# Seven quarter products for eight in the fp32 projection of a fused attention and SwiGLU kernel

## Chip, cores, metric

One NeuronCore of one Trainium2 chip. The metric is the device time of one execution in microseconds (us). Before the change it is 719.2 us (719.14 to 719.45). Each run of a changed kernel was made on the same chip as runs of the kernel before; the kernel before has medians of 718.9 to 719.2 us on these chips.

## The reference

```python
# attention: B=4, H=8, S=768, D=48; per head a state that decays by w
for t in range(S):
    cur = einsum('bhd,bhe->bhde', u * k[t], v[t])
    y[t] = einsum('bhd,bhde->bhe', r[t], state + cur)
    state = w[:, :, None] * state + einsum('bhd,bhe->bhde', k[t], v[t])
x = y.transpose(0, 2, 1, 3).reshape(3072, 384)
# feed-forward: d_model 384, d_ff 1536
g = x @ w_gate
h = (g * sigmoid(g)) * (x @ w_val)
return (h @ w_out).astype(float32)
```

The last product, `h @ w_out`, is what the change touches.

## The kernel before

The sequence is cut into 24 units of 128 tokens. The attention of unit s runs in step s. Two units make a group of 256 tokens, and the feed-forward of a group is cut into items that fill PE's gaps between the parts of the attention: twelve gate-and-value items and six projection items per group.

```python
def gate_value(g, f):                       # one item: 128 of the 1536 hidden columns
    gv = ps_f.tile([P, 2, 2 * P], FP32, name="gv", tag="gv")        # two PSUM buffers
    ...                                     # 3 + 3 matmuls of 256 columns
    act.activation(sg[:], gv[:, 0, :], AF.Sigmoid)
    dve.tensor_mul(sg[:], sg[:], gv[:, 0, :])
    dve.tensor_mul(hT[g][:, f, :], sg[:], gv[:, 1, :])              # frees gv

def project(g, j, part):                    # unit j of the group, a third of it
    ...
    for f in range(4 * part, 4 * part + 4):
        pe.matmul(ps[:], hT[g][:, f, P * j : P * (j + 1)], wo[:, f, :],   # 384 columns
                  start=(f == 0), stop=(f == FC - 1))
    if part == 2:
        act.copy(o_sb[:], ps[:])
        act.dma_start(out=out[n0 : n0 + P, :], in_=o_sb[:])
```

A step begins with work on POOL whose result DVE reduces. DVE takes its instructions in program order, so whatever follows `du` in the program waits with it:

```python
def own_product(i):
    pool.tensor_mul(rk[:], rl[:], kl[:])
    pool.tensor_mul(rk[:], rk[:], ub[:])
    dve.tensor_reduce(du[:], rk[:], axis=AX.X, op=ALU.add)

for s in range(3, N + 2):                   # conditions and queue() left out
    diagonal(s - 1)
    own_product(s + 1); scale(s + 1)        # POOL: rk, rk, khat, rhat
    turn(s); gaps(s, 0)                     # PE: two transposes tp; then fill items
    scores(s - 1, 0); gaps(s, 1)            # PE: s_ps; DVE: copy_predicated into At
    scores(s - 1, 1); gaps(s, 2)
    outputs(s - 2); gaps(s, 3)              # PE: y_ps
    update(s - 2); gaps(s, 4)               # PE: u_ps; DVE and POOL: Z
```

The tiles tp, s_ps, y_ps and u_ps share four PSUM banks. Steps 3 to 11 have few fill items (a step takes 13 us); later steps have twelve.

## Time and profile before

| | before |
|---|---|
| median time | 719.2 us |
| PE busy, share of the span | 97% |
| POOL busy, share | 21% |
| projection instructions on PE | 576, one per 322.5 ns |
| PE waits after 142 us | 0.6 us in all |

The lines behind this table stand in the prediction below. The page's first part gives each engine's busy time. Its second part cuts the span into 40 slices, with the busy share in tenths; `PEclk` is the clock granted to PE. A line of the timeline is start, length, engine, source line, operation, tiles, count. In brackets stands the idle time ahead of it with what ended it.

### The profile page before, as it was taken

To read this page: it belongs to the slowest core of one execution; us is meant where nothing else is said; L and a number is where in the kernel's file an instruction comes from. 1 tells how busy PE (TensorE), PEld (TensorE's weight loads), DVE (VectorE), ACT (ScalarE), POOL (GpSimd) and SP (SyncE) were. 2 spreads that over 40 slices of the span, in tenths; PEclk is the share of its full clock that TensorE was granted. 3 is DMA by queue.
4 is the path that set the end of the run, shared out by engine and by line. 5 is a ranking of instruction groups with operands and counts; after the bars stand their busy time and mean duration, and the time that the engine had idled before them with its cause. 6 is when DMAs were issued, how large, how long until landed. Compare 5 with 4: busy or idle time off the path is not lost.

```text
span 717.4 us, 10610 instructions
## 1 busy us (share of the span) xinstructions
PE 697.7 (97%) x4390; PEld 561.6 (78%) x4390; DVE 224.3 (31%) x479; ACT 202.2 (28%) x498; POOL 148.7 (21%) x143
## 2 busy tenths in 40 slices
PE   8878999999999999999999999999999999999996
PEld 8767888878778778788778788778778778778773
DVE  5777773312222223122213123213122213112120
ACT  3577764441213022313112212113122212111010
POOL 6877673250202020202020202020100000000000
PEclk9999999999999999999999999999999999999999
DMA  8798822121201010100111010110100000000000
GB/s 235 196 233 230 214 50 56 37 60 26 45 12 25 21 36 10 34 22 13 33 24 22 23 33 12 34 23 1 24 12 2 11 12 1 12 12 0 12 13 26
DMA packets 85770, 34.02 MB, mean 47 GB/s; under 512 B 76368, under 2 KB 79568, under 8 KB 85712
## 3 DMA queue, kind: packets, MB, share of 16 engines
q1 hardware_dynamic: 82256, 28.52, 17.2%
q10 hardware_dynamic: 3456, 4.72, 1.9%
q8 instruction: 37, 0.61, 0.4%
q14 instruction: 21, 0.17, 0.1%
HBM read 28.51 MB, written 4.72 MB: 46 GB/s over the span
## 4 chain that ended last, share of the span: by engine, by line
PE 86%; DVE 5%; ACT 5%; POOL 2%; issue 1%; DMA 1%; SPq 0%; DVEq 0%; POOLq 0%
PE gv L390 47%; PE o_ps L408 26%; PE y_ps L344 5%; PE s_ps L314 4%; PE tp L300 2%; ACT At L291 2%; PE u_ps L357 1%; ACT w_mag L162 1%; ACT kT L303 1%; DVE At L318 1%; DMA r_ld<-in_r_dram 1%; DVE wg L180 1%; DVE hT L398 1%; POOL At L285 1%; DVE wg L179 0%
## 5 line engine op out<-in xcount | busy, mean ns | idle before, releaser
L390 PE MATMUL gv<-xT,wg 128*128 128x256 f32 x864 | 212.3, 382 | 0.0
L390 PE MATMUL gv<-xT,wv 128*128 128x256 f32 x864 | 210.0, 379 | 0.0
L408 PE MATMUL o_ps<-wo,hT 128*128 128x384 f32 x576 | 198.0, 488 | 0.6 <-ACT o_sb L414 0.6
L397 DVE TENSOR_TENSOR sg<-sg,gv 128x256 f32<-128x256 f32 x144 | 60.5, 420 | 414.4 <-ACT sg L396 414.0
L390 PEld LDWEIGHTS gv<-xT,wg 128*128 128x128 f32 x864 | 160.0, 190 | 31.9 <-issue 1.8
L390 PEld LDWEIGHTS gv<-xT,wv 128*128 128x128 f32 x864 | 164.2, 190 | 22.3
L396 ACT ACTIVATE sg<-gv 128x256 f32<-128x256 f32 x144 | 55.1, 383 | 366.9 <-PE gv L390 366.8
L408 PEld LDWEIGHTS o_ps<-wo,hT 128*128 128x128 f32 x576 | 106.9, 190 | 63.7 <-issue 2.0
L370 POOL TENSOR_TENSOR Z<-Z,wL 96x384 f32<-96x384 f32 x16 | 15.9, 996 | 347.9 <-DVE Z L369 347.9
L398 DVE TENSOR_TENSOR hT<-sg,gv 128x256 f32<-128x256 f32 x144 | 60.5, 420 | 4.9
L291 ACT ACTIVATE At<-ident,du 128x128 f32<-128x128 f32 x176 | 53.6, 390 | 0.5 <-ACT o_sb L414 0.5
L314 PEld LDWEIGHTS s_ps<-rT,kT 96*128 96x128 f32 x384 | 49.2, 192 | 4.3 <-DVE At L318 1.6
L314 PE MATMUL s_ps<-rT,kT 96*128 96x128 f32 x384 | 50.5, 275 | 1.7 <-DVE At L318 1.3
L344 PE MATMUL y_ps<-At,v_ld 128*32 128x128 f32 x768 | 36.1, 279 | 6.5 <-ACT kT L303 5.2
L318 DVE COPY_PREDICATED At<-mask,s_ps 128x512 f32<-128x512 int32 x48 | 35.0, 731 | 5.0 <-PE s_ps L314 4.9
L344 PEld LDWEIGHTS y_ps<-At,v_ld 128*32 128x32 f32 x768 | 29.9, 111 | 7.5 <-ACT kT L303 5.6
L344 PE MATMUL y_ps<-rT,Z 96*32 96x128 f32 x480 | 30.2, 278 | 2.1 <-ACT kT L303 2.1
L414 ACT COPY o_sb<-o_ps 128x384 f32<-128x384 f32 x24 | 11.5, 479 | 72.7 <-PE o_ps L408 72.7
L303 ACT ACTIVATE kT<-tp,own 96x512 f32<-96x512 f32 x48 | 30.0, 675 | 3.6 <-PE tp L300 3.6
L162 ACT ACTIVATE w_mag<-w_bits 128x384 f32<-128x384 f32 x36 | 19.0, 528 | 24.9 <-DVE wg L180 10.8
L202 POOL TENSOR_TENSOR rk<-r_ld,k_ld 128x384 f32<-128x384 f32 x24 | 24.4, 1019 | 4.4 <-DMA r_ld<-in_r_dram 4.4
L344 PEld LDWEIGHTS y_ps<-rT,Z 96*32 96x32 f32 x480 | 19.3, 109 | 7.6 <-issue 4.6
(57 smaller groups left out, 347.4 us busy)
## 6 DMA issues: line engine op xcount, KB each, us to landing
k_ld<-in_k_dram SPq DMA_DIRECT2D x24, 192.0 KB, 2.8
r_ld<-in_r_dram SPq DMA_DIRECT2D x24, 192.0 KB, 3.5
w_bits<-in_moe_w_gate_dram SPq DMA_DIRECT2D x6, 768.0 KB, 5.1
v_ld<-in_v_dram SPq DMA_DIRECT2D x48, 96.0 KB, 2.8
w_bits<-in_moe_w_val_dram SPq DMA_DIRECT2D x6, 768.0 KB, 5.0
w_bits<-in_moe_w_out_dram SPq DMA_DIRECT2D x6, 768.0 KB, 4.5
out_dram<-o_sb ACTq DMA_DIRECT2D x24, 192.0 KB, 1.9
ub<-in_u_dram SPq DMA_DIRECT2D x1, 192.0 KB, 4.2
```

The source lines that it names most:

```text
L162: act.activation(mags[n][-1].bitcast(FP32), hi.bitcast(FP32), AF.Abs, scale=float(2.0**-112))
L202: pool.tensor_mul(rk[:], rl[:], kl[:])
L291: act.activation(At[i % 2][:, h, :], ident[:], AF.Identity, scale=du[:, h : h + 1])
L303: act.activation(kT[i % 2][:, :, e, :], tp[0:D2], AF.Identity, scale=own[:, e : e + 1])
L314: pe.matmul(ps[:, n, :], kT[i % 2][:, a, e, :], turned[i][:, a, :], start=True, stop=True, skip_group_check=True,)
L318: dve.copy_predicated(At[i % 2][:, 4 * half : 4 * half + 4], mask[:].bitcast(INT32).unsqueeze(1).to_broadcast([P, HP, P]), ps[:],)
L344: pe.matmul(ps[32 * q : 32 * q + 32, cc, :], *rows[q][n], start=(n == 0), stop=(n == len(rows[q]) - 1), skip_group_check=True,)
L390: pe.matmul(gv[:, o, :].rearrange("p (i t) -> p i t", i=2), wt[:, c, P * f : P * (f + 1)], xT[:, 2 * g % NX : 2 * g % NX + 2, c, :], start ...
L396: act.activation(sg[:], gv[:, 0, :], AF.Sigmoid)
L397: dve.tensor_mul(sg[:], sg[:], gv[:, 0, :])
L398: dve.tensor_mul(hT[g][:, f, :], sg[:], gv[:, 1, :])
L408: pe.matmul(ps[:], hT[g][:, f, P * j : P * (j + 1)], wo[:, f, :], start=(f == 0), stop=(f == FC - 1),)
```

## The change

The projection of a group is a product of a 256 x 1536 matrix by a 1536 x 384 one. Cut in quarters it takes eight products of 128 x 768 by 768 x 192. A form of Strassen's algorithm needs seven, with sums of quarters on both sides: four weight sums (once; one of them overwrites its quarter, `w12`) and four hidden sums per group. Everything stays fp32. The sums go to POOL, those of the last group to DVE.

```diff
+    def weight_sums():
+        pool.tensor_sub(wt[1][:], w22, w12)
+        pool.tensor_sub(w12, w12, w11)
+        pool.tensor_sub(wt[0][:], w22, w12)
+        pool.tensor_sub(wt[2][:], w21, wt[0][:])
+    def h_sums(g, by):
+        ...
+        by.tensor_add(s1, h22, h21)
+        by.tensor_sub(s2, s1, h11)
+        by.tensor_sub(s3, h11, h21)
+        by.tensor_sub(s4, h12, s2)
...
-    def project(g, j, part):
-        for f in range(4 * part, 4 * part + 4):
-            pe.matmul(ps[:], hT[g][:, f, P * j : P * (j + 1)], wo[:, f, :], ...)
+    def project(g, n):                     # product n of seven, accumulators a and b
+        ...
+        lhs, rhs, acc = ((h11, w11, "a"), (h12, w21, "b"), (s2, wt[0], "a"), (s3, wt[1], "a"),
+                         (s1, w12, "b"), (h22, wt[2], "a"), (s4, w22, "b"))[n]
+        for f in range(FH):
+            pe.matmul(ps[:], lhs[:, f, :], rhs[:, f, :], ...)      # 192 columns
+        ...                                # 4 ACT copies and 3 DVE adds per group
...
+            todo.append((NW + 1, lambda: h_sums(0, pool)))         # a fill item; so for each group
...
         gaps(s, 4)
         if s == 12:
             count_outside()
+        if done["pool"] == NW and not summed:
+            summed.append(True)
+            weight_sums()                  # at the end of step 7, ahead of the next rk
```

More of the change, by code (lines that the diff above doesn't have):

```diff
@@ L398, in gate_value @@
         dve.tensor_mul(hT[g][:, f, :], sg[:], gv[:, 1, :])
-    o_ps = {}
-    def project(g, j, part):
-        c, b = divmod(2 * g + j, B)
-        if part == 0:
-            o_ps[g, j] = ps_o.tile([P, DM], FP32, name="o_ps", tag="o")
-        ps = o_ps[g, j]
-        for f in range(4 * part, 4 * part + 4):
+    FH, NH = FC // 2, DM // 2
+    w11, w12, w21, w22 = (
+        wo[:, FH * k : FH * (k + 1), NH * n : NH * (n + 1)] for k in range(2) for n in range(2)
+    )
+    wt = [cst.tile([P, FH, NH], FP32, name=f"wt{n}") for n in (2, 3, 4)]
@@ new lines, in weight_sums, with h_quarters @@
+    def weight_sums():
[3 more added lines that the diff above has]
+        pool.tensor_sub(wt[2][:], w21, wt[0][:])
+    part_of = {}
+    def h_quarters(g):
+        return [
+            hT[g][:, FH * k : FH * (k + 1), P * j : P * (j + 1)] for j in range(2) for k in range(2)
+        ]
+    def h_sums(g, by):
+        a, b = (
+            three.tile([P, 2, FH, P], FP32, name=n, tag="w_bits") for n in ("hs12", "hs34")
+        )
+        h11, h12, h21, h22 = h_quarters(g)
+        s1, s2, s3, s4 = a[:, 0], a[:, 1], b[:, 0], b[:, 1]
+        by.tensor_add(s1, h22, h21)
+        by.tensor_sub(s2, s1, h11)
+        by.tensor_sub(s3, h11, h21)
+        by.tensor_sub(s4, h12, s2)
+        part_of[g] = {"s": (s1, s2, s3, s4)}
@@ new lines, in project @@
+    def project(g, n):
+        h11, h12, h21, h22 = h_quarters(g)
+        x = part_of[g]
+        if n == 0:
+            x["a"] = ps_o.tile([P, NH], FP32, name="o_a", tag="o")
+            x["b"] = ps_w.tile([P, NH], FP32, name="o_b", tag="w_mag")
+            x["out"] = [two.tile([P, DM], FP32, name="o_sb", tag="o_sb") for _ in range(2)]
+        s1, s2, s3, s4 = x["s"]
+        lhs, rhs, acc = (
+            (h11, w11, "a"), (h12, w21, "b"), (s2, wt[0], "a"), (s3, wt[1], "a"),
+            (s1, w12, "b"), (h22, wt[2], "a"), (s4, w22, "b"),
+        )[n]
+        ps = x[acc]
+        for f in range(FH):
@@ L408, in project @@
             pe.matmul(
-                ps[:], hT[g][:, f, P * j : P * (j + 1)], wo[:, f, :],
-                start=(f == 0), stop=(f == FC - 1),
-            )
-        if part == 2:
-            o_sb = two.tile([P, DM], FP32, name="o_sb", tag="o_sb")
-            act.copy(o_sb[:], ps[:])
+                ps[:], lhs[:, f, :], rhs[:, f, :],
+                start=(f == 0 and n in (0, 1, 4)), stop=(f == FH - 1), skip_group_check=True,
+            )
+        o1, o2 = x["out"]
+        if n in (0, 2, 3):
+            nm = {0: "p1", 2: "u2", 3: "u3"}[n]
+            x[nm] = two.tile([P, NH], FP32, name=nm, tag=nm)
+            act.copy(x[nm][:], ps[:])
+        elif n == 1:
+            dve.tensor_add(o1[:, 0:NH], x["p1"][:], ps[:])
+        elif n == 4:
+            dve.tensor_add(o2[:, NH:DM], x["u3"][:], ps[:])
+        elif n == 5:
+            act.copy(o2[:, 0:NH], ps[:])
+        else:
+            dve.tensor_add(o1[:, NH:DM], x["u2"][:], ps[:])
@@ L415, in project @@
+        if n >= 5:
+            j = 6 - n
+            c, b = divmod(2 * g + j, B)
             n0 = S * b + P * c
-            act.dma_start(out=out[n0 : n0 + P, :], in_=o_sb[:])
+            act.dma_start(out=out[n0 : n0 + P, :], in_=x["out"][j][:])
+    summed = []
     todo = []
@@ L422, in feed @@
         for _ in range(n):
-            ready = [k for k, (need, _) in enumerate(todo) if need <= done["pool"]]
+            ready = [k for k, (need, _) in enumerate(todo) if need <= done["pool"] + len(summed)]
             if ready:
@@ L427, in queue @@
     def queue(g):
-        parts = [(NW, lambda p=p: project(g - 1, p // 3, p % 3)) for p in range(6)] if g > 1 else []
+        parts = [(NW + 1, lambda p=p: project(g - 1, p)) for p in range(7)] if g > 1 else []
         if g == 2:
-            todo.extend((NW, lambda p=p: project(0, p // 3, p % 3)) for p in range(6))
+            todo.append((NW + 1, lambda: h_sums(0, pool)))
+            todo.extend((NW + 1, lambda p=p: project(0, p)) for p in range(7))
         for f in range(FC):
-            need = 2 * (f // 2) + 2 if g < 2 else NW
+            need = 2 * (f // 2) + 2 if g < 2 else NW + 1
             todo.append((need, lambda f=f: gate_value(g, f)))
-            if parts and 2 <= f < 8:
+            if parts and f == 0:
+                todo.append((NW + 1, lambda: h_sums(g - 1, pool)))
+            if parts and 2 <= f < 9:
                 todo.append(parts.pop(0))
@@ L509, in fast @@
             count_outside()
+        if done["pool"] == NW and not summed:
+            summed.append(True)
+            weight_sums()
     assert done["pool"] == NW
     feed(len(todo))
-    for p in range(6):
-        project(N // 2 - 1, p // 3, p % 3)
+    h_sums(N // 2 - 1, dve)
+    for p in range(7):
+        project(N // 2 - 1, p)
 @with_exitstack
```

## The prediction

> **What bounds the kernel now.** I read the page's busy shares first, then the slices and the chain of waits, to see whether one engine sets the end throughout.
>
> ```profile
> PE 697.7 (97%) x4390; PEld 561.6 (78%) x4390; DVE 224.3 (31%) x479; ACT 202.2 (28%) x498; POOL 148.7 (21%) x143
> PE   8878999999999999999999999999999999999996
> POOL 6877673250202020202020202020100000000000
> PEclk9999999999999999999999999999999999999999
> PE 86%; DVE 5%; ACT 5%; POOL 2%; issue 1%; DMA 1%; SPq 0%; DVEq 0%; POOLq 0%
> L408 PE MATMUL o_ps<-wo,hT 128*128 128x384 f32 x576 | 198.0, 488 | 0.6 <-ACT o_sb L414 0.6
> ```
>
> PE is full in every slice after the sixth. The list of waits from 142 us to the end holds only one wait of PE, 0.6 us, between the last two units. So after 142 us a microsecond of PE work taken out is a microsecond of the end, unless it returns as a wait. The projection is 576 instructions. POOL, which gets the new work, is idle most of the time, but it is in order, and so is DVE behind it.
>
> The 488 ns of the row is latency; what counts is the spacing of starts. I took it from PE's timeline in a full stretch:
>
> ```profile
> 403.51 2.74 PE L408 MATMUL o_ps<-wo,hT 128*128 128x384 f32 x8
> 406.09 0.84 PE L357 MATMUL u_ps<-v_ld,khat 128*96 128x96 f32 x8
> 406.76 1.49 PE L390 MATMUL gv<-xT,wg 128*128 128x256 f32 x6
> ...
> 420.60 1.06 PE L314 MATMUL s_ps<-rT,kT 96*128 96x128 f32 x8
> 421.49 2.75 PE L408 MATMUL o_ps<-wo,hT 128*128 128x384 f32 x8
> ```
>
> (406.09-403.51)/8 = 322.5 ns for 384 columns; 0.67/8 = 84 ns for 96; 0.89/8 = 111 ns for 128; L390 (six in 1.29 to 1.30 us, next rows) 215.8 ns for 256. The line through 256 and 384 is 0.833 ns per column plus 2.5 ns, and 96 and 128 lie within 2 ns of it.
>
> **What the Trainium skill says.** (1) "TensorE: Matmul & The Clock Gate", section "Back-to-back issue gap": an isolated warm matmul takes N/2.4 + 2.5 ns. Here the slope is twice that (322.5 ns = 2 x 384/2.4 + 2.5), and each matmul of the program stands as two instructions in the trace (576 for 288). That fits (2) "FP8 and Floating Point Precision", section "TensorE Precision Notes": true FP32 is four passes. So fp32 is stream bound, with almost no fixed part, and halving the columns halves the time. The weight load is a separate 190 ns record, but s_ps starts every 111 ns with a new 128-column stationary each time, so at 162 ns it stays hidden. (3) "GPSIMD Engine Reference", section "Elementwise — side-by-side cycle accounting": a two-input fp32 operation of 2048 elements took 4497 ns. The trace agrees in rate: 384 elements take 1.01 us (L202 to L275), 768 int32 ones 1.87 us (L190). (4) the first page, section "What's actually happening": an idle window of about 3.4 us halves PE's clock. The trace shows it: PE is idle from 51.0 to some 55.6 us, and the stretch 56 to 58 us has a granted clock of 0.50.
>
> **The change, part by part.**
>
> *Removed and added on PE.* Before, a group is 2 units x 12 blocks x 2 instructions = 48 at 322.5 ns = 15.48 us. After, 7 products x 6 blocks x 2 = 84 at 192 columns, 0.833 x 192 + 2.5 = 162.5 ns, = 13.65 us. That is 1.83 us a group, 12 groups: **-22.0 us**.
>
> *Evacuation.* One ACT copy of 384 columns per unit (0.479 us) becomes four ACT copies and three DVE adds of 192 per group, about 0.32 and 0.35 us each (my scaling of 256 in 0.383 and 0.420). Both engines are under a third busy. There is one buffer per accumulator, so product 3 must wait for the copy after product 2 on the same one. In the built order there is in nearly all groups a gate-and-value item (2.59 us of PE) or attention work between them. The tightest are three groups where eight diagonal activations and three copies stand before that ACT copy: it ends some 5.0 us into the step and is needed at 5.4. The last group has the products adjacent and pays about 0.55 us, as the old one did between its units. I allow **+0.7 us** for all of it.
>
> *Sums of hidden tiles on POOL.* Four operations of 768 elements, some 1.8 us each with 0.1 us after a dependent one: 7.4 us a group. From group 1 on I placed them by the built order: they stand after that step's scaling work, or at the end of a step in which khat and rhat for the next are already made, and product 2 comes over 10 us later. Nothing waits. The last group's run on DVE (about 0.9 us each): sums 1 and 2 end 3.4 us after PE's last gate-and-value matmul, and products 0 and 1 cover 3.9 us.
>
> *Weight sums, once.* Four operations of 1152 elements, about 2.6 us each (estimate from the 384 and 768 rows), with dependences 10.7 us. They stand on POOL between Z and the next rk, when the last chunk of wo is rounded. This is where I looked at POOL and DVE together:
>
> ```profile
> 104.09 0.99 POOL L370 TENSOR_TENSOR Z<-Z,wL 96x384 f32<-96x384 f32 x1 [0.92 <-DVE Z L369]
> 105.04 0.99 POOL L202 TENSOR_TENSOR rk<-r_ld,k_ld 128x384 f32<-128x384 f32 x1
> 106.11 1.00 POOL L203 TENSOR_TENSOR rk<-rk,ub 128x384 f32<-128x384 f32 x1
> ```
>
> ```profile
> 107.15 0.55 DVE L205 TENSOR_REDUCE du<-rk 128x8 f32<-128x384 f32 x1 [0.31 <-POOL rk L203]
> 107.62 0.73 DVE L318 COPY_PREDICATED At<-mask,s_ps 128x512 f32<-128x512 int32 x1
> 110.33 0.42 DVE L397 TENSOR_TENSOR sg<-sg,gv 128x256 f32<-128x256 f32 x1 [1.97 <-ACT sg L396]
> 110.78 0.42 DVE L398 TENSOR_TENSOR hT<-sg,gv 128x256 f32<-128x256 f32 x1
> ```
>
> ```profile
> 107.12 1.46 PE L390 MATMUL gv<-xT,wg 128*128 128x256 f32 x6
> ...
> 112.39 1.56 PE L390 MATMUL gv<-xT,wg 128*128 128x256 f32 x6
> ...
> 115.76 1.49 PE L390 MATMUL gv<-xT,wg 128*128 128x256 f32 x6
> ```
>
> DVE takes du in program order, and du needs rk. With the sums ahead, rk ends 10.7 us later and du starts at 107.15 + 10.7 = 117.85. Behind du stand the copy (0.47 after it), sg (0.63) and hT (0.46 + 0.42): hT frees the gv buffer of the item at 107.12 at about 119.85. There are two gv buffers, so the items at 107.12 and 112.39 go, and the third, at 115.76, waits: **+4.1 us** on PE. An idle of that length may or may not hold a whole clock window; the one of 4.6 us did, and cost some 1.5 us (about 3 us at half clock). I count **+0.5 us**.
>
> *First group's hidden sums.* They also stand at a step's end, after Z at 143.19, before the next rk. From 144.15 they end near 151.6, rk at 153.6, du, then the two copies of At at 154.8 and 155.4, which free the buffers of the next transposes; khat and rhat are ready at 154.6 and 155.5. PE, with its three products at 1.95 us, reaches those transposes at 152.75 and would end them at 153.6; it ends them at 156.0: **+2.4 us**. Steps are short here (13 us, three fill items), later they are 27 us, which is why only these two bite.
>
> Sum: 719.24 - 21.96 + 4.1 + 0.5 + 2.4 + 0.7 = 705.0. I put 705.2.
>
> **Rivals.** *PE work is not stream bound at 192 columns* (weight loads bind). For it: a load record is 190 ns, longer than 162.5; were that the spacing, a group would cost 84 x 190 = 16.0 us, more than before, and the time would be 725 or more. Against it: the 111 ns of s_ps. I give it 2%. *POOL's in-order work hits every group*, through DVE's du: some 2.5 us x 11 would make 727. Against it: the built order puts later sums mid-step, and PE holds 27 us of work a step; I give 5% to half of this. *No stall at all:* POOL's operations are faster (L285, 1024 elements with broadcast inputs, took 1.90 us) or PE has more slack than I see: 719.2 - 22.0 + 0.7 = 698. About 10% for coming near it. *Single accumulators stall on ACT* in each group by 0.5 us: +6, 711; 10%.
>
> **Range and chances.** The saving on PE is known to some 0.3 us; the two stalls (6.5 us together) to perhaps 2 us; clock and small waits to 1.5 us. So 702.0 to 708.6 for eight in ten. Two per cent is 704.9, almost at my number. Faster 0.44, same 0.55, slower 0.01.
>
> **What would show it.** Right: the group of projection matmuls counts 1008 instructions with starts 162 to 163 ns apart; PE busy falls by about 22 us; PE has a wait near 115.8 us of 4 us ended by DVE's hT, another near 157 us (clock of after) of 2.4 us ended by khat, rhat or At, and hardly any later; POOL's share rises by 11 x 7.4 + 10.7 = 92 us. Wrong: spacing near 190 ns; a PE wait repeating with each group; ACT copies as releasers of PE; the sums at other durations than 1.8 and 2.6 us; or the wait at 115.8 us missing, which would mean that I misread what DVE's order holds back.

## The result, and the profile after

| | before | after |
|---|---|---|
| median time | 719.2 us | 708.0 us (707.04 to 708.13) |
| ratio | | 0.984 (0.982 to 0.986) |
| mean granted clock of the profiled run | 0.997 | 0.988 |
| PE busy | 697.7 us | 681.0 us |
| POOL busy | 148.7 us | 237.1 us |

A ratio is the mean time of one kernel's fast runs over that of the other's of the same rounds, so not quite the ratio of the medians quoted. The time fell by 1.6%: inside the range on record, 2.8 us above its centre, and inside the 2% that were to separate "faster" from "same". The result is correct.

The page of the changed kernel, its busy times, slices and chain:

```profile
PE 681.0 (96%) x4822; PEld 620.2 (88%) x4822; DVE 240.7 (34%) x519; ACT 204.4 (29%) x522; POOL 237.1 (34%) x191
PE   8888997999899999999999999999999999999996
PEclk9998998999999999999999999999999999999999
PE 81%; DVE 6%; POOL 5%; ACT 5%; issue 1%; DMA 1%; SPq 0%; DVEq 0%; POOLq 0%
```

PE's row now has slices below 9 in the first third, the clock dips there, and POOL has entered the chain with 5% where it had 2%. The waits of PE from 100 us on (total, times, longest):

```profile
PE gv L390 <- DVE hT L398: 4.0, 1, 4.0
PE n_ps L378 <- DVE ones L376: 1.8, 1, 1.8
PE tp L300 <- DVE At L318: 1.7, 1, 1.7
PE o_a L453 <- ACT u L461: 0.4, 1, 0.4
```

Four waits, each once, and none that repeats with each group. The largest can be read across three engines' timelines, POOL first, then DVE, then PE:

```profile
104.83 2.62 POOL L414 TENSOR_TENSOR wt<-wo 128x1152 f32<-128x1152 f32 x1
...
115.54 0.99 POOL L202 TENSOR_TENSOR rk<-r_ld,k_ld 128x384 f32<-128x384 f32 x1
```

```profile
117.63 0.55 DVE L205 TENSOR_REDUCE du<-rk 128x8 f32<-128x384 f32 x1 [11.00 <-POOL rk L203]
118.10 0.71 DVE L318 COPY_PREDICATED At<-mask,s_ps 128x512 f32<-128x512 int32 x1
118.72 0.40 DVE L397 TENSOR_TENSOR sg<-sg,gv 128x256 f32<-128x256 f32 x1
119.15 0.42 DVE L398 TENSOR_TENSOR hT<-sg,gv 128x256 f32<-128x256 f32 x1
```

```profile
119.72 2.90 PE L390 MATMUL gv<-xT,wg 128*128 128x256 f32 x6 [4.00 <-DVE hT L398]
122.41 2.77 PE L390 MATMUL gv<-xT,wv 128*128 128x256 f32 x6
124.97 0.85 PE L300 MATMUL tp<-ident,khat 128*96 128x128 f32 x4
```

The four weight sums hold POOL from 104.8 to 115.5 us. DVE stands idle for 11.0 us ahead of du, and hT, three instructions behind it, ends at 119.57. PE starts its item at 119.72, 4.0 us late. But the wait is not the whole loss: the item's two halves start 2.69 and 2.56 us apart, where 1.30 us is usual. The view by stretches says why (length, then busy time of PE, its weight loads, DVE, ACT, POOL; then clock, DMA share, GB/s):

```profile
116.00:118.00 2.00, 0.00 (x0) 0.00 (x0) 0.37 (x1) 0.00 (x0) 1.92 (x3) 1.00 0.00 0
118.00:120.00 2.00, 0.28 (x1) 0.31 (x2) 1.97 (x5) 0.00 (x0) 1.51 (x2) 0.66 0.12 22
120.00:122.00 2.00, 2.00 (x6) 1.56 (x6) 1.39 (x4) 0.00 (x0) 0.49 (x1) 0.50 0.96 187
```

The clock fell to one half while PE was idle and came back in the stretch from 124 to 126 us. From 119.72 to the second transpose at 125.66 PE took 5.94 us for what takes 2.59 + 0.44 = 3.03 us: 2.9 us lost, besides the 4.0 us. This is the gate of the skill's page "TensorE: Matmul & The Clock Gate", section "What's actually happening", which gives an idle window of about 3.4 us. The trace agrees only roughly: here the clock fell 2.9 us after PE went idle (115.7 to 118.7), and half clock lasted 6.8 us, to 125.5. Shorter waits, of 2.9 and 1.8 us, were followed by half clock too, as ws_halves and the open point further down show.

The spacing of the new matmuls, from PE's timeline near the end:

```profile
694.96 2.11 PE L453 MATMUL o_b<-wo,hs 128*128 128x192 f32 x12
...
696.91 2.11 PE L453 MATMUL o_a<-wt,hT 128*128 128x192 f32 x12
```

Twelve instructions in 1.95 us, 162.5 ns each, with a weight load ahead of every one.

### The profile page after: what moved, and what is told of

Same layout as the page of the kernel before. It is cut to its first block, busy times and chain, and to the rows that moved or that the text cites. A ratio compares the mean times of both kernels' runs of the same rounds, so it can differ in the third digit from the quotient of the medians.

```text
span 706.3 us, 11610 instructions
## 1 busy us (share of the span) xinstructions
PE 681.0 (96%) x4822; PEld 620.2 (88%) x4822; DVE 240.7 (34%) x519; ACT 204.4 (29%) x522; POOL 237.1 (34%) x191
## 4 chain that ended last, share of the span: by engine, by line
PE 81%; DVE 6%; POOL 5%; ACT 5%; issue 1%; DMA 1%; SPq 0%; DVEq 0%; POOLq 0%
PE gv L390 47%; PE o_a L453 13%; PE o_b L453 10%; PE y_ps L344 4%; PE s_ps L314 4%; PE tp L300 2%; ACT At L291 2%; ACT w_mag L162 1%; PE u_ps L357 1%; DVE At L318 1%; ACT kT L303 1%; DVE hT L398 1%; DVE sg L397 1%; DVE wg L180 1%; DMA r_ld<-in_r_dram 1%
## 5 line engine op out<-in xcount | busy, mean ns | idle before, releaser
L390 PE MATMUL gv<-xT,wg 128*128 128x256 f32 x864 | 216.0, 387 | 4.0 <-DVE hT L398 4.0
L432 POOL TENSOR_TENSOR hs<-hT 128x768 f32<-128x768 f32 x11 | 19.9, 1809 | 195.6 <-DVE hT L398 195.6
L453 PE MATMUL o_a<-wt,hs 128*128 128x192 f32 x288 | 50.9, 327 | 0.4 <-ACT u L461 0.4
L453 PE MATMUL o_b<-wo,hs 128*128 128x192 f32 x288 | 50.7, 326 | 0.0
L453 PEld LDWEIGHTS o_a<-wt,hs 128*128 128x128 f32 x288 | 47.5, 190 | 1.5 <-ACT u L461 0.7
L453 PEld LDWEIGHTS o_b<-wo,hs 128*128 128x128 f32 x288 | 47.6, 190 | 0.8
```

Source lines behind the costliest of these rows:

```text
L390: pe.matmul(gv[:, o, :].rearrange("p (i t) -> p i t", i=2), wt[:, c, P * f : P * (f + 1)], xT[:, 2 * g % NX : 2 * g % NX + 2, c, :], start ...
L432: by.tensor_add(s1, h22, h21)
L453: pe.matmul(ps[:], lhs[:, f, :], rhs[:, f, :], start=(f == 0 and n in (0, 1, 4)), stop=(f == FH - 1), skip_group_check=True,)
```

## The experiments

The theory: PE saves its stream time in full. What comes back is (a) one wait caused by POOL's weight sums, carried to PE by DVE's in-order wait for du; (b) the clock that falls during this wait; (c) two smaller waits in the first group's steps. The rivals: narrow matmuls cost more than their stream; POOL's work costs PE wherever it stands; the clock fell for another reason. Ten kernels were run. "Changed kernel" is the kernel after the change, at 708.0 us.

### Narrowness alone: eight_quarters

The kernel before, each matmul split in two of 192 columns; no sums, no product saved.

```diff
-        for f in range(4 * part, 4 * part + 4):
-            pe.matmul(ps[:], hT[g][:, f, ...], wo[:, f, :], ...)
+        for nf in range(8 * part, 8 * part + 8):
+            n, f = divmod(nf, FC)
+            cols = slice(NH * n, NH * (n + 1))
+            pe.matmul(ps[:, cols], hT[g][:, f, ...], wo[:, f, cols], ...)
```

> Edit: the kernel before, each matmul of 384 columns replaced by two of 192 (1152 projection instructions in the trace for 576), no sums, no seventh product saved. The cost of narrowness alone. Stream-bound theory: 96 x 163 ns = 15.65 us a group against 48 x 322.5 = 15.48, so 719.2 + 12 x 0.17 = 721 us. Rival (each further weight load of 190 ns shows): 96 x 190 = 18.2 us a group, 752 us.

Measured: 721.4 us (two runs, 720.97 and 721.78), against 718.9 of its rounds: +2.5 us for 576 more instructions on PE. So twelve groups of eight quarter products cost 12 x 15.48 + 2.5 = 188.3 us, or 163.4 ns per instruction, all transitions included. Weight loads do not bind at 192 columns. With seven products the stream falls by 12 x (15.48 - 84 x 0.1634) = 21.1 us, which is 0.9 us less than the prediction's 22.0.

### The sums alone: sums_only

The kernel before with its old projection, and the sums on POOL at the places that the change gives them, into tiles nobody reads.

```diff
+    wt = [cst.tile([P, FH, NH], FP32, name=f"wt{n}") for n in (2, 3, 4, 5)]
+    def weight_sums():                      # as in the change, but w12 is left as it is
+    def h_sums(g, by):                      # as in the change
+            todo.append((NW + 1, lambda: h_sums(0, pool)))          # and one for each later group
+        if done["pool"] == NW and not summed:
+            summed.append(True)
+            weight_sums()
```

> Edit: the kernel before, its projection of eight products of full width kept, with the weight sums and hidden sums of the change added on POOL at the same places (into tiles nobody reads; w12 is left as it is). The cost of the sums alone. Theory: the gv wait of 4.0 us and the 2.9 us of half clock come, and a small rest for the first group's step (its three products ahead are 2.6 us long here, so the 1.7 us wait all but vanishes): 719.2 + 6.9 + 0 to 1 = 726 to 727 us. Rival (the sums cost nothing and the change lost its gain in the products): 719 to 720.

Measured: 726.8 us (726.12 to 727.67), +7.9 us. The longest line of PE's waits from 90 us on shows where:

```profile
PE gv L390 <- DVE hT L398: 4.9, 3, 3.9
```

The long one, 3.9 us, is the one of the changed kernel, and the item behind it again shows halves of 2.70 and 2.56 us. The two others come to 1.0 us together. So the sums by themselves cost some 8 us of the 21 that the products save.

### Is it the delay, and with what slack: ws_double, ws_halves, ws_midstep, ws_rotate

In the changed kernel du came 10.7 us late and PE waited 4.0 us, so POOL should have a slack of 6.7 us at this place. First the dose was doubled: the first weight sum is repeated four times more.

```diff
     def weight_sums():
+        for _ in range(4):
+            pool.tensor_sub(wt[1][:], w22, w12)
         pool.tensor_sub(wt[1][:], w22, w12)
```

> Edit: the first weight sum is repeated four times more, so 8 operations (some 21.4 us) stand where 4 (10.7 us) stood; results unchanged. Theory A: the wait on PE is POOL's delay less a slack of 6.7 us, so 4.0 becomes 4.0 + 10.7 = 14.7 us, with the clock lost once as before (some 2.9 us): 708.0 + 10.7 = 718.7 us. Rival B (a share of the length): a wait of about 8 us, 712. If the half clock lasts longer after a longer idle time: above 719.

Measured: 718.5 us (717.65 to 718.98). The gv wait:

```profile
PE gv L390 <- DVE hT L398: 14.8, 1, 14.8
```

The wait grew by 10.8 us for 10.7 us more work: behind the slack, POOL's time is PE's time, one for one. The clock was lost once, as before; an idle time nearly four times as long did not cost more of it: half clock ended at 136.0 us, 5.2 us after the item started (5.8 us in the changed kernel).

Then the dose was halved: two sums at the end of step 7, two at the end of step 8.

```diff
-        if done["pool"] == NW and not summed:
-            summed.append(True)
-            weight_sums()
+        if s in (7, 8):
+            weight_sums(s - 7)              # two of the four operations
+            if s == 8:
+                summed.append(True)
```

> Edit: the four weight sums split, two at the end of the step where all four stood and two one step later; nothing else. Theory A (POOL's delay reaches PE through DVE's in-order wait for du, with a slack): in the changed kernel du came 10.7 us late and hT freed the gv buffer at 119.6 us while PE wanted it at 115.6; without the delay it would have been free at 108.9, so the slack is 6.7 us. Half the work is 5.4 us at each place, under the slack: both waits 0, and no idle stretch that halves the clock. PE's 4.0 us wait and the 2.9 us of half clock behind it vanish: 708.0 - 6.9 = 701.1 us. Rival B (any work on POOL at that place costs PE its length or a share of it): the waits become two of some 2 us, total unchanged near 706 to 708. Rival C (the wait is real, the half clock has another cause): 704.

Measured: 712.7 us (712.0 to 713.4). This missed by 11.6 us, and on the wrong side. The longest waits of PE from 90 us on:

```profile
PE y_ps L344 <- DVE At L318: 5.8, 2, 2.9
PE n_ps L378 <- DVE ones L376: 1.8, 1, 1.8
...
```

The gv wait is gone, so the slack for this carrier is real. Another carrier took its place, twice: y_ps now waits for the copy into At, which stands directly behind du. The built program shows the reason. The four PSUM banks of the attention tiles are not taken in strict turn. In step 8 of the changed kernel, where its du is late, y_ps got the bank of the step's first transpose, which ACT frees early; in steps 8 and 9 of this build, where its du is late, y_ps got the bank of the first score tile, which is freed by the copy behind du. The slack of that path is shorter: 5.4 us of delay less 2.9 us of wait leave some 2.5. Each of the two waits was again followed by lost clock (the mean in the stretches 100 to 120 us and 130 to 142 us was 0.91 and 0.86): 3.4 us at half clock, which costs 1.7 us.

Two runs settle this. One places the halves where no du is behind them, after rk, khat and rhat of steps 8 and 9:

```diff
             own_product(s + 1)
             scale(s + 1)
+        if s in (8, 9):
+            weight_sums(s - 8)
+            if s == 9:
+                summed.append(True)
```

> Edit: the weight sums in two halves of 5.4 us, each placed behind the step's rk, khat and rhat on POOL (two steps in a row), so that no du waits for them; POOL was idle for 8.1 us there. The run of halves at the steps' ends showed 712.7: y_ps waited twice 2.9 us for the copy into At behind du, since the builder gave y_ps the PSUM bank of the step's first score tile. Theory A (it is only the delay of du that reaches PE, by whatever buffer): no wait for hT or At before the first group's step, the clock stays: 708.0 - 4.0 - 2.9 = 701.1 us. Rival (POOL's length counts wherever it stands): 706 or more.

Measured: 701.0 us (700.92 to 702.77), ratio 0.976. The other keeps the halves at the steps' ends and takes the banks in strict turn:

```diff
-    ps_a = ctx.enter_context(tc.tile_pool(name="ps_a", bufs=4, ...))
+    ps_a = ctx.enter_context(tc.tile_pool(name="ps_a", bufs=1, ...))
+    def bank():
+        count[0] += 1
+        return f"a{count[0] % 4}"
...
-        ps = ps_a.tile([P, HP, P], FP32, name="s_ps", tag="a")
+        ps = ps_a.tile([P, HP, P], FP32, name="s_ps", tag=bank())      # so for tp, y_ps, u_ps
```

> Edit: halves at the steps' ends as in the run that gave 712.7, but the four PSUM banks of the attention tiles are taken in strict turn (four tags of one buffer), so y_ps has the bank of the step's first transpose and not that of the first score tile. Theory A with the bank as the carrier: the two y_ps waits of 2.9 us and the clock lost behind them vanish, the gv buffer is freed by hT with 1 us to spare: 701 us. Rival (half the work at the step's end costs PE in any case): 706 to 713.

Measured: 701.8 us (700.76 to 702.81), with no wait of y_ps for At and none of gv. The same sums at the same place cost 11 us by the medians (9.2 us between the two profiled runs, which is two waits of 2.9 us with 1.7 us of clock each) or nothing, by the banks that the attention tiles got. Both runs keep the 1.7 and 1.8 us waits, as they should.

### Is DVE's order the carrier: du_late

The changed kernel, with the reduction to du issued at the end of its step. The weight sums stay where they are.

```diff
-            own_product(s + 1)
+            own_product(s + 1, late=True)   # POOL's part only
...
         gaps(s, 4)
+        if later:
+            later.pop()()                   # dve.tensor_reduce(du, rk)
```

> Edit: the reduction of rk to du on DVE is issued at the end of its step and no longer at its start; weight sums and hidden sums stay as in the changed kernel. Theory A (DVE stands behind du, and du behind POOL): the 4.0 us wait of gv for hT vanishes with the half clock, PE then comes to the transposes at about 118.2 us, khat is ready at 118.6 and rhat at 119.5: waits of some 0.9 us appear there. The wait of the first group's step (1.7 us, for At) turns into one for khat and rhat of about 1.7 us, since these end at 161.2 and 162.2. So 708.0 - 6.9 + 0.9 = 702 us. Rival (POOL itself, not DVE's order, holds PE): waits stay 4 us or more, 707 to 708.

Measured: 702.7 us (702.4 to 704.19), ratio 0.978. PE's timeline at the place of the old wait, and the two longest waits from 90 us on:

```profile
117.22 1.46 PE L398 MATMUL gv<-xT,wv 128*128 128x256 f32 x6
118.98 0.64 PE L308 MATMUL tp<-ident,khat 128*96 128x128 f32 x4 [0.30 <-POOL khat L282]
119.94 0.64 PE L308 MATMUL tp<-ident,rhat 128*96 128x128 f32 x4 [0.32 <-POOL rhat L283]
```

```profile
PE n_ps L386 <- DVE ones L384: 2.1, 1, 2.1
PE tp L308 <- POOL khat L282: 1.6, 2, 1.3
...
```

POOL is as busy as before, and only 0.6 us of direct waits for it are left here. In the first group's step the wait for At became one for khat, 1.3 us, and one for rhat, 0.3 us, as expected.

### Is the rest the clock: warm_fill

The changed kernel, with matmuls nobody reads in front of the item that waits.

```diff
+        if s == 8:
+            fill = ps_o.tile([P, NH], FP32, name="fill", tag="o")
+            for _ in range(18):
+                pe.matmul(fill[:, 0:P], ident[:], ident[:], start=True, stop=True)
         gaps(s, 4)
```

> Edit: 18 warm-up matmuls of 128 columns (36 instructions of 0.111 us, 4.0 us together) into a PSUM tile nobody reads, placed just ahead of the gate-and-value item that waits 4.0 us. POOL, DVE and the wait's cause are as in the changed kernel. Theory (half the loss is the clock that drops after the idle stretch): PE never idles, the granted clock stays 1.00 from 118 to 126 us, the two halves of that item take 1.30 us each and not 2.69 and 2.56: 708.0 - 2.9 = 705.1 us. Rival (clock drops for another reason, or the loss is only the wait): 708.

Measured: 705.6 us (705.23 to 707.08).

```profile
115.55 4.21 PE L572 MATMUL fill<-ident 128*128 128x128 f32 x36
119.73 1.53 PE L390 MATMUL gv<-xT,wg 128*128 128x256 f32 x6
121.10 1.46 PE L390 MATMUL gv<-xT,wv 128*128 128x256 f32 x6
122.39 0.60 PE L300 MATMUL tp<-ident,khat 128*96 128x128 f32 x4
```

The item starts at 119.73, exactly as late as without the fill (119.72), since hT is what it waits for. But it takes 2.66 us and not 5.25, and the granted clock is 1.00 from 116 to 126 us. Extra work of no use made the kernel 2.4 us faster. That separates the wait (4.0 us) from the clock (2.4 us by time, 2.9 by the timeline). The profiled run, 707.1 us, is the slowest of the four: at u_ps of step 9 it is 2.8 us ahead of the changed kernel (132.13 against 134.96), and it loses 1.7 us behind the wait of n_ps, as the open point below tells.

### The two smaller waits: hs0_mid and best

hs0_mid is ws_midstep with the first group's hidden sums also placed mid-step, in steps 10 and 11, and no longer a fill item at the end of step 10.

```diff
-            todo.append((NW + 1, lambda: h_sums(0, pool)))
...
             scale(s + 1)
+        if s == 10:
+            h_sums(0, pool)                 # s1 and s2
+        if s == 11:
+            part_of[0]["rest"]()            # s3 and s4
```

> Edit: the kernel with the weight sums mid-step (701.0), and the first group's hidden sums in two halves behind the scaling work of the two steps before, in place of a fill item at the end of a step. Theory: du of the next step is no longer late, and the 1.7 us wait of the transposes for At goes: 701.0 - 1.7 = 699.3 us; the 1.8 us wait of n_ps stays. Rival (the transposes wait for something else, or the wait moves to the next tile): 701.

Measured: 699.0 us (698.2 to 699.75), ratio 0.973. The wait for At is gone. The wait of n_ps fell to 0.3 us by itself, which was not expected: without the hidden sums in the list, the fill item ahead of n_ps is a product (at 183.01 us) and no gate-and-value item, and DVE is further ahead.

best adds one thing: the three small DVE operations of the count of out-of-range values are issued a step before the matmul that uses them.

```diff
+        if s == 11:
+            compare_outside()               # dve: bad, badc, ones
         if s == 12:
             count_outside()                 # pe and act only
```

> Edit: as the run beside it, and the three small DVE operations of the count of values out of range are issued one step earlier than its matmul. Theory: the 1.8 us wait of n_ps for DVE goes as well, PE has no wait above 0.5 us after 100 us: 719.0 - 21.5 + 0.1 = 697.6 us, 3.0% under the kernel before, nearly the whole saving of PE's stream. Rival (the wait of n_ps hides another, of the transposes behind it for khat): 699.

Measured: 697.7 us (697.6 to 698.29), ratio 0.971 (0.969 to 0.972): 3.0% faster than the kernel before, 1.5% faster than the changed kernel. It is correct. All waits of PE from 90 us on:

```profile
PE y_ps L344 <- ACT kT L303: 0.5, 1, 0.5
PE o_a L463 <- ACT u L471: 0.4, 1, 0.4
```

Its gain on hs0_mid is 1.2 us by medians, more than the 0.3 us wait it removes. Between the two profiled runs (698.72 and 698.29 us) it is 0.4; the rest lies in runs without a profile and stays open. The clock in the first 60 us, whose mean goes from 0.92 to 0.97 in the profiles, does not explain it: in all twelve profiles u_ps of step 7 starts at 101.75 to 102.19 us, at 102.14 and 102.18 in these two.

## Why the prediction was right, and where it was off

- **PE is stream bound and the saving is its columns.** Right. The predicted 162.5 ns is the spacing within a product; with all transitions eight_quarters gives 163.4 ns, and the saving is 21.1 us, not 22.0.
- **The weight sums hold PE once, through DVE's du.** Right in mechanism and size: predicted 4.1 us, measured 4.0; POOL's operations were to take 2.6 us and took 2.62 to 2.64. du_late shows the carrier, ws_double the one-for-one rule. One premise was luck, and the prediction doesn't even name it: that no attention tile waits for a bank behind du before gv does. ws_halves shows that a build can give y_ps a bank that makes the same delay cost far more.
- **The clock.** This is the term that was mis-sized. I counted +0.5 us, as a chance of a loss of 1.5. The trace shows 2.9 us, and warm_fill 2.4 by time. The kernel before had shown the same thing after 4.45 us of idle PE (4.6 in the prediction), so counting it in full was open to me.
- **The first group's hidden sums.** Predicted 2.4 us, measured 1.7.
- **Not foreseen: the wait of n_ps, 1.8 us.** The new order of fill items put a gate-and-value item ahead of that small matmul. Its sigmoid and DVE products come before the three operations that n_ps needs. I had walked through the transposes and not through this one.
- **ACT copies between products on one accumulator.** Predicted +0.7 us, measured one wait of 0.4, in place of the old 0.6: -0.2.
- **Later groups' sums do not reach PE.** Right: no wait from 200 us to the last group. The slack was larger than argued: a later step is 36 us long (its u_ps starts 36.3 us after the last one in the kernel before), not 27.
- **PE busy falls by about 22 us.** It fell by 16.7, from 697.7 to 681.0. PE is counted as busy at half clock too: 2.9 us more behind the long wait and 2.1 us more in the first 100 us (87.9 us busy against 85.8). In best, without the long wait, it fell by 21.6.
- **A slip in a rival.** Stalls of 2.5 us in 11 groups, on top of the prediction's other terms for the weight sums, make 730, not 727; nothing rests on it.

The sum with measured terms: 719.2 - 21.1 + 4.0 + 2.9 + 1.7 + 1.8 - 0.2 = 708.3, against 708.0 measured. The 2.8 us between 705.2 and 708.0 are the clock (2.4), n_ps (1.8) and narrowness (0.9), less the terms that came out smaller (1.7 in all) and some 0.6 us of rounding and of what the sum does not hold.

Open: the four or five runs of one changed kernel spread over 0.7 us (best) to 2.1 us (ws_rotate), where those of the kernel before stay within 0.5. A part of this can be read in the traces. In the profiles of ws_halves, ws_rotate and warm_fill the 1.8 us wait of n_ps is followed by 3.4 us at half clock, which costs 1.7 us; in those of the changed kernel, ws_double, ws_midstep and du_late it is not. From warm_fill:

```profile
190.93 0.19 PE L378 MATMUL n_ps<-ones,badc 96*1 96x1 f32 x2 [1.82 <-DVE ones L376]
...
192.32 3.43 PE L453 MATMUL o_a<-wt,hs 128*128 128x192 f32 x12
```

The next instruction starts 3.27 us after this product did; in the changed kernel it is 1.96 us. So a wait that costs 1.8 us in one execution can cost 3.5 in another. What decides it, no run shows. It is not the whole spread either: in hs0_mid this wait is 0.3 us, and its runs spread over 1.6 us.

## What to carry to other kernels

When PE is full, count a cut in its work by spacing and columns, and then ask for each piece of new work on another engine which in-order queue stands behind it and which buffer that queue frees. Put such work behind the operations that others wait for, not ahead of them, and check which bank each tile got in the build, since a slack belongs to one carrier only. A PE wait can cost more than its length: here 4.0 us cost 2.4 to 2.9 us more in clock, and 1.8 us cost 1.7 us more in some executions. If such a wait can't be removed, filling it with idle matmuls can pay, as it did here.

## What the Trainium skill lacked or had wrong

- "TensorE: Matmul & The Clock Gate", section "Back-to-back issue gap": no spacing for fp32. The runs show two instructions per matmul, each 322.5 ns at 384 columns, 215.8 at 256, 162.5 at 192 and 111 at 128, that is 2N/2.4 + 2.5 ns to within 2 ns.
- Same page, section "The mechanism": its list of what overlaps says that a weight load overlaps running matmuls only when the row group differs, while the text above that list and the section "Step-by-step: what each phase is for" also let it go ahead into a background weight buffer. The runs agree with the second: here every load and matmul of the projection uses all 128 rows, the load is recorded with 190 ns, and matmuls still start every 162.5 ns. The section "LDWEIGHTS (loading the stationary operand)" would give 107 ns for the load (an estimate from its formula with 128 columns); the fp32 record is 190.
- Same page, section "What's actually happening": it lets the clock fall after at least one idle window of about 3.4 us. The runs show half clock after waits of 2.9 us as well (ws_halves, twice), and after 1.8 us in three of the seven profiles that have this wait. The cost of one wait here: 4.0 us of idle PE cost 2.4 to 2.9 us more, 14.8 us no more than that, 2.9 and 1.8 us cost 1.7 us each where the clock fell.
- "GPSIMD Engine Reference", section "Elementwise — side-by-side cycle accounting": only 2048 elements (4497 ns) are given for a two-input fp32 operation. Measured: 1.01 us at 384, 1.81 at 768, 2.63 at 1152, which is 2.1 ns for each further element, against 4497/2048 = 2.2 ns.
- No page tells that the bank which a tile gets when the kernel is built can decide whose delay reaches PE: the same work at the same place gave 712.7 and 701.8 us.
